# One store of attention's output and a copy by DMA, other queues for the last stores, and new plan numbers in an attention and mixture-of-experts kernel

## The chip, the cores and the metric

The kernel runs on one core of one Trainium2 chip. The metric is the device time of one execution in microseconds (us), the median of several runs. The kernel before takes 1061.25 us (three runs, 1060.74 to 1063.13).

## What is computed

Attention over 8 batches, 8 heads, 576 tokens and 64 columns a head, in which each query keeps its 32 largest scores, and behind it a mixture of 8 experts over all 4608 tokens. A token takes part only if its skip score is above zero, and goes to one expert.

```python
scores = scale * np.matmul(q, k.transpose(0, 1, 3, 2))
kth = np.partition(scores, -top_k, axis=-1)[..., -top_k:-top_k + 1]     # top_k = 32
scores = np.where(scores >= kth, scores, -1e9)
attn = np.exp(scores - max); attn /= sum + 1e-9
x = np.matmul(attn, v) -> rows of 512 columns, one row a token

do_compute = x @ w_skip > 0
e_idx = argmax(xc @ w_gate)                       # xc: the rows with do_compute
y[e_idx == e] = gate_w * (relu(xc @ w1[e]) @ w2[e])
out = x, and xc + y in the rows with do_compute
```

## The kernel before

Attention works on 32 pairs of heads (p), 4 pairs to a batch. For each pair, `load` and `load_v` bring q, k and v in (L85, L86, L505 to L510), `prep` turns q and k (L561) and swaps halves by DMA (tile TS, L584, L586), `rows` makes the scores of 9 row blocks (L619), finds each row's 32nd value with VectorE (L690 to L698), and marks the rest through ScalarE (L703, L716), GpSimd (L706, L710, L714) and VectorE (L719). `units` makes the scores again, turned and masked (L758 to L809), and `heads` multiplies by v (L850, L857), divides (L860, L888, L863, into the tile xb) and adds up the router's logits (L867 to L873).

The output of a pair goes from xb twice to DRAM: to XD, the table from which the experts gather their tokens, and to out. Each is one task `put` of four DMAs on SP's queue (L913, L914). For the last pair `put_last` (L906, L908) puts XD's four on ScalarE's queue and out's four on SP's.

When the four batches 0 to 3, the three batches 4 to 6, or batch 7 are complete, `route` ranks their tokens among the experts (L400 to L442), stores the gate weights into XD (`store`, L353 and L354; on ScalarE's queue for batch 7, else on SP's), and `lists`, once a batch, builds one-hots (rrh L461 and L466, lo1 in five parts L470) which TensorE multiplies into lists of tokens (L476, added up by VectorE at L479). For batches 0 to 6 the one-hots of L466 and L470 are GpSimd's; for batch 7 three of five parts and L466 are VectorE's (the function `on`).

The first two blocks of expert 0 need only batches 0 to 6: they are gathered on GpSimd (`gather`, L1026), turned (L1045, L1049 on ScalarE, L1053 on VectorE) and multiplied (`up` L1110 to L1112, `down` L1133 to L1135). Its third block and the other experts wait for batch 7's lists. The weights are split into two parts for the products by `part_hi` (L963, ScalarE) and `part_lo` (L966, VectorE), and fetched by L960 on SP. Expert outputs go to out by an indirect scatter (L1039).

The order on every engine is fixed when the kernel is built. A planner (`Plan`, `pick`, `run`) plays the work through with a duration and a due time for each task; each engine takes, of the tasks ready first, the one due first, and issues its instructions in that order. Due times are 9 a pair, plus a number for the kind of task (K, FINE); LOOK and GAIN say when an engine may wait for a more urgent task, TURN what a change of TensorE's kind of product costs. There are two runs of the plan: one ends with attention and the turning of expert 0's first blocks, the second holds batch 7's route, expert 0 and the turning for expert 1. Engines execute in order, and SP, which issues nearly all DMAs, waits in order too.

Of the kernel before, what the change touches and what calls it, by code (L numbers as in the profile page):

```python
# [32 lines left out]
LOOK, GAIN, KEEP = 0.027, 36.005, 0.000  # L33
DRAIN, TURN = 0.11, 28700.19
K = dict(ld=-546.563, turn=-120.465, put=-237.977, swap=-421.948, rr=33.73, rc=-49.731, qk=42.376, copy=-177.435, chunk=76.184, step=11.097, cand=-62.556, cstep=-187.113, sign=-8.081, fill=-185.335, push=-553.097, window=-5.964, pen=333.292, top=-210.867, flag=-156.199, unit=143.314, exp=-190.441, f1=70.038, f5=-98.317, lg=-208.068, co=298.059, ce=-33.501, rt=406.078, rd=63.598, rs=-191.199, moe=493.198, vt=-35.892, vp=-215.869, vg=-230.983, lv=-174.638, lr=-8.41)

FINE = dict(turn=(-249.498, -433.994, -337.654), put=(351.929, -329.073, -660.94), swap=(-41.128, -119.866, -577.692, -199.011), qk=(187.823, -221.268, 505.088, 511.446, 108.203), copy=(-246.306, -73.921, 287.494, -108.704, -278.328), chunk=(-24.303, -6.103, -7.999, 33.525, -39.857, -37.824, 1.877, 20.048, -67.673), cand=(5.33, -41.889, -480.491, -501.067, -1.709, -9.738, -282.518, -57.751, 36.539), sign=(481.767, 179.764, 7.521, 236.037, 144.293, 55.588, 387.412, 201.445, 493.783), fill=(4.812, -185.534, 211.624, 6.001, 13.752, 10.699, -0.796, 170.396, -154.693), push=(89.009, -290.332, 343.332, -115.781, 149.083, -72.663, -444.053, 220.923, -636.945), window=(-214.222, -578.183, 110.655, -507.736, -338.509, 68.646, 54.63, -121.054, -200.803), pen=(197.017, 233.591, -609.792, 155.04, 161.382, -368.212, 123.195, -300.258, 86.571), top=(132.194, 180.552, 274.851), unit=(-176.43, -402.794, 3.19, 161.712, 223.085, 129.562), exp=(-215.454, 342.652, -375.644, -329.678, 283.567, -477.568), f1=(102.089, -312.556, -403.168, -107.097, 72.352, -290.717, -487.223, 19.781, -483.104, 57.113, -224.605), f5=(-518.292, -303.227, -99.179, -77.179, -205.205, -250.298), lg=(372.735, -10.653), vt=(63.521, 158.904), vp=(-309.717, 192.783), vg=(-158.098, 364.353))
RS = 1.0
FILLS = True
# [4 lines left out]
def tile_kernel(ctx, tc, q, k, v, w_skip, w_gate, w1, w2, out):  # L44
# [303 lines left out]
    def store(b, xb, whats, due, after, end=False):  # L348

        q = nc.scalar if end else nc.sync  # L350

        def f(dst, u, w):
            q.dma_start(dst[b * S:b * S + MAIN, u:w].rearrange("(p t) c -> p t c", p=P), xb()[:, 0:NM])  # L353
            q.dma_start(dst[b * S + MAIN:(b + 1) * S, u:w], xb()[0:REM, NM])  # L354
        return [pl.add("ACT" if end else "SP", 0.15 if end else 1.35, due, lambda x=x: f(*x), after, lag=2.5) for x in whats]

    def route(bs, wk, due, bank=BT):
# [88 lines left out]
        on = lambda late: ("DVE", 0.2, V_) if late and end else ("POOL", 0.61, nc.gpsimd)  # L446
        listed = [None, None, bx]

        def lists(j):
# [14 lines left out]
            for k, a in enumerate((ta, tb)):  # L464
                e, dur, eng = on(True)
                u.append(pl.add(e, min(dur, 0.39), due, lambda k=k, a=a, eng=eng: eng.tensor_tensor(  # L466
                    L["rh"][:, :, k], L["rh"][:, :, 2], bl(a), op=OP.mult), x))
# [214 lines left out]
    def row(p, t):  # L682
# [52 lines left out]
        fx = A("POOL" if FILLS else "DVE", 0.25 if FILLS else 0.129, W_("fill"), fill, rr, old)  # L735
# [91 lines left out]
    def heads(p):  # L827
# [10 lines left out]
        def values(a):  # L838
# [53 lines left out]
            for j in range(4 if a else 1):  # L892
                x = A(on, 0.1 if end else 0.25, when(p, "lg", a), lambda j=j: logit(j), x, LGFREE[-1:])
                LGFREE.append(x)
                logits.append(x)
# [8 lines left out]
        def put_last(dst, a, q):  # L904
            c0 = hp * P + a * D
            q.dma_start(dst[b * S:b * S + MAIN, c0:c0 + D].rearrange("(p t) d -> p t d", p=P), xb[:, a, 0:NM, 0:D])  # L906
            for h in range(2) if a else ():
                q.dma_start(dst[b * S + MAIN:(b + 1) * S, hp * P + h * D:hp * P + (h + 1) * D], xb[hs_(h), 1, NM, 0:D])  # L908

        def put(dst):  # L910
            q, c0 = nc.sync, hp * P
            for h in range(2):
                q.dma_start(dst[b * S:b * S + MAIN, c0 + h * D:c0 + (h + 1) * D].rearrange("(p t) d -> p t d", p=P), xb[:, h, 0:NM, 0:D])  # L913
                q.dma_start(dst[b * S + MAIN:(b + 1) * S, c0 + h * D:c0 + (h + 1) * D], xb[hs_(h), 1, NM, 0:D])  # L914
        if end:
            STORES[p] = [A("ACT", 0.6 + 1.2 * a, due, lambda a=a: put_last(XD, a, nc.scalar), done[a], lag=2.5) for a in range(2)]
            for a in range(2):
                A("SP", 0.6 + 1.2 * a, due, lambda a=a: put_last(out, a, nc.sync), STORES[p][a], lag=2.5)
        else:
            STORES[p] = [A("SP", 1.35, due, lambda dst=dst: put(dst), done, lag=2.5) for dst in (XD, out)]  # L920
# [583 lines left out]
```

## Time and profile before

| | us |
|---|---|
| median of three runs | 1061.25 |
| the profiled execution, its own time | 1061.84 |
| its span, from the first to the last instruction | 1059.9 |
| TensorE busy | 1004.0 |
| VectorE busy | 898.6 |
| ScalarE busy | 862.2 |
| GpSimd busy | 706.7 |

Attention takes the span up to about 804 us, the experts the rest. A busy share over the whole span mixes the two: in attention TensorE, VectorE and ScalarE are all nearly full, behind it TensorE alone is. In the rows below, times are microseconds from the start of the span; in a row of the timeline the first number is the start, the second the duration, x how many instructions are merged, and the bracket at the end how long the engine stood idle before it and what released it. PE is TensorE, DVE VectorE, ACT ScalarE, POOL GpSimd, SPq and ACTq the DMA issues of SyncE and ScalarE.

### The profile page before, as it was taken

How to read it: one execution, taken by the hardware profiler on the slowest of the kernel's cores; microseconds unless marked ns; L12 is line 12 of the kernel's file. 1: busy time of each engine (PE TensorE's matmuls, PEld its weight loads, DVE VectorE, ACT ScalarE, POOL GpSimd, SP SyncE). 2: the span in 40 equal slices, each digit the busy share in tenths (PEclk: the TensorE clock that was granted, in tenths of full speed). 3: DMA queues.
4: the chain of work that ended last, by engine and by line, in shares of the span. 5: the costliest groups of instructions: out<-in, count | busy, mean ns of one | idle time of the engine just before them, and what ended most of it. 6: DMA issues, size and time to landing. Idle time of an engine off the chain costs nothing.

```text
span 1059.9 us, 40100 instructions
## 1 busy us (share of the span) xinstructions
PE 1004.0 (95%) x14932; PEld 714.4 (67%) x14932; DVE 898.6 (85%) x4914; ACT 862.2 (81%) x1548; POOL 706.7 (67%) x1074
## 2 busy tenths in 40 slices
PE   6889999999999999998999899999997999999996
PEld 3456666666666657665666566666676999888995
DVE  5999999999999999997999899999875666674661
ACT  5999999999999999997999899999993354434540
POOL 3878878888777888886779898888993222210210
PEclk9899999999999999998999899999998999999998
DMA  4433444444444434434354444554226275554720
GB/s 111 98 85 80 92 95 96 91 105 97 97 94 94 92 90 100 104 86 87 88 120 113 114 105 98 118 131 90 60 49 198 74 249 168 169 161 165 210 80 29
DMA packets 290092, 116.16 MB, mean 110 GB/s; under 512 B 258920, under 2 KB 275304, under 8 KB 289888
## 3 DMA queue, kind: packets, MB, share of 16 engines
q1 hardware_dynamic: 283504, 103.42, 39.9%
q0 software_dynamic: 3360, 9.47, 2.7%
q8 instruction: 120, 1.97, 0.8%
q10 hardware_dynamic: 3024, 0.61, 0.3%
q14 instruction: 84, 0.69, 0.2%
HBM read 76.91 MB, written 24.53 MB: 96 GB/s over the span
## 4 chain that ended last, share of the span: by engine, by line
PE 54%; DVE 14%; POOL 13%; ACT 11%; issue 4%; DMA 2%; SPq 1%; ACTq 0%; POOLq 0%; DVEq 0%
PE r L619 7%; POOL xw L706 7%; PE r L767 6%; DVE cand L690 6%; PE pa L850 5%; PE pt L850 4%; PE ph L1110 4%; PE ph L1111 4%; PE ph L1112 4%; DVE wn L719 3%; PE py L1133 3%; PE py L1135 3%; ACT r L703 3%; PE py L1134 3%; POOL xw L710 2%
## 5 line engine op out<-in xcount | busy, mean ns | idle before, releaser
L706 POOL TENSOR_TENSOR xw<-XC,r 128x576 f32<-128x576 f32 x288 | 364.8, 1281 | 84.1 <-ACT r L703 53.6
L690 DVE MAX8 cand<-XC 128x8 f32<-128x82 f32 (+1 forms) x2016 | 359.1, 229 | 15.1 <-ACT XC L647 14.4
L703 ACT ACTIVATE r<-XC,cl 128x576 bf16<-128x576 f32 x288 | 226.4, 793 | 7.0 <-DVE cl L696 3.4
L719 DVE MAX8 wn<-xw 128x8 f32<-128x585 f32 x288 | 215.0, 760 | 16.6 <-POOL xw L710 13.4
L619 PE MATMUL r<-TT 64*64 64x64 f32 (+1 forms) x1280 | 198.8, 426 | 1.6 <-ACT PTM L800 0.8
L716 ACT ACTIVATE PEN<-XC,wn 128x576 bf16<-128x576 f32 x225 | 171.5, 791 | 3.0 <-DVE wn L719 2.5
L619 PE MATMUL r<-TS 64*64 64x512 f32 (+1 forms) x1024 | 158.8, 422 | 3.1 <-DMA TS<-TT 3.1
L696 DVE MAX8 cl<-cand 128x8 f32<-128x42 f32 (+2 forms) x864 | 158.1, 191 | 0.9
L767 PE MATMUL r<-TT 64*128 64x512 f32 (+1 forms) x528 | 147.8, 638 | 9.2 <-ACT XC L649 7.4
L800 ACT ACTIVATE PTM<-r,top 128x1024 f32<-128x1024 f32 x124 | 137.3, 1123 | 4.0 <-PE r L758 3.9
L647 ACT ACTIVATE XC<-r 128x1024 f32<-128x1024 f32 x128 | 132.0, 1037 | 7.0 <-PE r L619 6.8
L758 PEld LDWEIGHTS <-PEN 64*128 64x128 bf16 (+1 forms) x2880 | 70.9, 99 | 72.9 <-issue 68.3
L714 POOL TENSOR_SCALAR PEN<-XC,wn 128x576 bf16<-128x576 f32 x63 | 108.8, 1729 | 12.9 <-DVE wn L719 2.7
L710 POOL TENSOR_SCALAR xw<-wo,CN 128x9 f32<-128x9 f32 x288 | 98.6, 343 | 26.0
L698 DVE MATCH_REPLACE8 cand<-cl,cand 128x28 f32<-128x28 f32 (+1 forms) x576 | 102.0, 180 | 0.0
L850 PEld LDWEIGHTS pa<-VG,PTM 128*64 128x64 f32 x2048 | 72.6, 138 | 28.1 <-ACT PTM L800 5.7
L850 PEld LDWEIGHTS pt<-VG,PTM 128*64 128x64 f32 x2048 | 72.7, 138 | 27.5 <-ACT PTM L800 8.0
L619 PEld LDWEIGHTS r<-TT 64*64 64x64 f32 x1280 | 59.5, 134 | 45.2 <-issue 29.0
L1110 PE MATMUL ph<-xh,hi 128*128 128x224 f32 (+4 forms) x288 | 85.9, 298 | 3.6 <-DVE xl L1053 3.6
L850 PE MATMUL pt<-VG,PTM 128*64 128x74 f32 x2048 | 83.3, 232 | 3.5 <-DVE xb L863 1.7
L850 PE MATMUL pa<-VG,PTM 128*64 128x74 f32 x2048 | 83.8, 232 | 2.8 <-DVE xb L863 1.7
L1026 POOL DMA_INDIRECT xg<-xd,idx x21 | 23.3, 1112 | 93.9 <-DVE ot L1032 85.3
(257 smaller groups left out, 2058.8 us busy)
## 6 DMA issues: line engine op xcount, KB each, us to landing
wb<-in_moe_w_dram SPq DMA_DIRECT2D x32, 512.0 KB, 7.3
raw<-in_moe_w_dram SPq DMA_DIRECT2D x28, 512.0 KB, 3.4
TS<-TT SPq DMA_DIRECT2D x64, 144.0 KB, 2.5
raw<-in_k_dram SPq DMA_DIRECT2D x64, 128.0 KB, 3.2
VG<-in_v_dram SPq DMA_DIRECT2D x64, 128.0 KB, 2.6
vraw<-in_v_dram SPq DMA_DIRECT2D x64, 128.0 KB, 2.7
out_dram<-xb SPq DMA_DIRECT2D x64, 128.0 KB, 2.3
raw<-in_q_dram SPq DMA_DIRECT2D x62, 128.0 KB, 2.7
```

The costliest lines, as they stand in the source:

```text
L619: nc.tensor.matmul(o[hs_(h)], q_, (ts[src, u:w] if y else tt[src, 0, u:w]), start=True, stop=True)
L647: nc.scalar.activation(xc[:, t:u + 1:u - t, 0:MAIN], h2.t.rearrange("p (y c) -> p y c", y=2), AF.Copy)
L690: nc.vector.max(C_[:, c], xc[:, CH[c]:CH[c + 1]])
L696: nc.vector.max(L[:, 4 * r:4 * r + 8], c)
L703: nc.scalar.activation(rr_, xc, AF.Sign, bias=CL[p % 2][:, t, 23:24], scale=-ODD, accum_out=CN[:, s:s + 1])
L706: nc.gpsimd.tensor_tensor(xw[:, 0:S], xc, rr_, op=OP.mult)
L716: nc.scalar.activation(pen, xc, AF.Relu, bias=WN[p % 2][:, t, 7:8], scale=-1.0)
L719: nc.vector.max(WN[p % 2][:, t], xw)
L767: nc.tensor.matmul(rb[:, 512 * h + u:512 * h + w], tt[hs_(h), 0, REM + P * kc:REM + P * (kc + 1)], tt[hs_(h), 1, REM + u:REM + w], start=T ...
L800: nc.scalar.activation(o_.rearrange("p h c -> p (h c)"), i_, AF.Exp, bias=nb, scale=scale)
L850: nc.tensor.matmul(h.t[hs_(t % 2), VW * (t // 2):VW * (t // 2 + 1)], w, vg[:, a, kc], start=(kc == 0 and t < 2), stop=(kc == NM), skip_gro ...
L1110: nc.tensor.matmul(ph[:, u:w], h1[:, c], xh[:, c, u:w], start=(c == 0), stop=False)
```

## The change

A pair's output is stored once, to XD: one DMA as soon as the first half of xb is done, three DMAs for the second half. A further task on SP copies the pair's 576 rows of 128 columns from XD to out with one DMA from DRAM to DRAM, which waits for those stores and is due 12 behind them. The last pair has no stores of its own kind any more; they and batch 7's gate stores are on SP. The one-hots of L466 and of three of the five parts of L470 are VectorE's for batches 4 to 6 too. The plan's durations for several tasks are set to other values (fill, logits, one-hots, stores), and all its due numbers and LOOK, GAIN and TURN are new.

```diff
-LOOK, GAIN, KEEP = 0.027, 36.005, 0.000
-DRAIN, TURN = 0.11, 28700.19
+LOOK, GAIN, KEEP = 0.026, 6.352, 0.000
+DRAIN, TURN = 0.11, 86667984302.89
...
-        q = nc.scalar if end else nc.sync
+        q = nc.sync
...
-        return [pl.add("ACT" if end else "SP", 0.15 if end else 1.35, due, lambda x=x: f(*x), after, lag=2.5) for x in whats]
+        return [pl.add("SP", 0.15 if end else 1.35, due, lambda x=x: f(*x), after, lag=2.5) for x in whats]
...
-        on = lambda late: ("DVE", 0.2, V_) if late and end else ("POOL", 0.61, nc.gpsimd)
+        on = lambda late: ("DVE", 0.2, V_) if late and b0 + nb >= B - 1 else ("POOL", 0.61, nc.gpsimd)
...
-                u.append(pl.add(e, min(dur, 0.39), due, lambda k=k, a=a, eng=eng: eng.tensor_tensor(
+                u.append(pl.add(e, dur if end else 0.36 if e == "POOL" else 0.25, due, lambda k=k, a=a, eng=eng: eng.tensor_tensor(
...
-        fx = A("POOL" if FILLS else "DVE", 0.25 if FILLS else 0.129, W_("fill"), fill, rr, old)
+        fx = A("POOL" if FILLS else "DVE", 0.40 if FILLS else 0.129, W_("fill"), fill, rr, old)
...
-                x = A(on, 0.1 if end else 0.25, when(p, "lg", a), lambda j=j: logit(j), x, LGFREE[-1:])
+                x = A(on, 0.1 if end else 0.28, when(p, "lg", a), lambda j=j: logit(j), x, LGFREE[-1:])
...
-        def put_last(dst, a, q):
+        def put(a):
             c0 = hp * P + a * D
-            q.dma_start(dst[b * S:b * S + MAIN, c0:c0 + D].rearrange("(p t) d -> p t d", p=P), xb[:, a, 0:NM, 0:D])
+            nc.sync.dma_start(XD[b * S:b * S + MAIN, c0:c0 + D].rearrange("(p t) d -> p t d", p=P), xb[:, a, 0:NM, 0:D])
             for h in range(2) if a else ():
-                q.dma_start(dst[b * S + MAIN:(b + 1) * S, hp * P + h * D:hp * P + (h + 1) * D], xb[hs_(h), 1, NM, 0:D])
-
-        def put(dst):
-            q, c0 = nc.sync, hp * P
-            for h in range(2):
-                q.dma_start(dst[b * S:b * S + MAIN, c0 + h * D:c0 + (h + 1) * D].rearrange("(p t) d -> p t d", p=P), xb[:, h, 0:NM, 0:D])
-                q.dma_start(dst[b * S + MAIN:(b + 1) * S, c0 + h * D:c0 + (h + 1) * D], xb[hs_(h), 1, NM, 0:D])
-        if end:
-            STORES[p] = [A("ACT", 0.6 + 1.2 * a, due, lambda a=a: put_last(XD, a, nc.scalar), done[a], lag=2.5) for a in range(2)]
-            for a in range(2):
-                A("SP", 0.6 + 1.2 * a, due, lambda a=a: put_last(out, a, nc.sync), STORES[p][a], lag=2.5)
-        else:
-            STORES[p] = [A("SP", 1.35, due, lambda dst=dst: put(dst), done, lag=2.5) for dst in (XD, out)]
+                nc.sync.dma_start(XD[b * S + MAIN:(b + 1) * S, hp * P + h * D:hp * P + (h + 1) * D], xb[hs_(h), 1, NM, 0:D])
+
+        def copy_out():
+            bs, cs = slice(b * S, (b + 1) * S), slice(hp * P, (hp + 1) * P)
+            nc.sync.dma_start(out[bs, cs], XD[bs, cs])
+        STORES[p] = [A("SP", 0.62 + 1.24 * a, due, lambda a=a: put(a), done[a], lag=2.5) for a in range(2)]
+        A("SP", 0.64, due + 12.0, copy_out, STORES[p], lag=2.5)
```

## Rows read from the trace of the kernel before

**Rows 1.** The page's busy times: time, share of the span, instructions of each engine.

```profile
PE 1004.0 (95%) x14932; PEld 714.4 (67%) x14932; DVE 898.6 (85%) x4914; ACT 862.2 (81%) x1548; POOL 706.7 (67%) x1074
```

**Rows 2.** Busy time of engines by stretch, with length, granted clock, DMA share, GB/s.

```profile
100.00:400.00 300.00, 292.88 (x5281) 190.46 (x5279) 291.72 (x1815) 297.82 (x546) 247.41 (x355) 1.00 0.43 95
400.00:760.00 360.00, 346.49 (x6196) 225.10 (x6192) 340.24 (x2105) 345.75 (x634) 303.92 (x461) 0.98 0.45 103
490.00:510.00 20.00, 15.58 (x252) 10.20 (x248) 12.92 (x86) 13.04 (x26) 11.93 (x19) 0.83 0.49 105
590.00:610.00 20.00, 16.96 (x278) 11.40 (x271) 17.89 (x111) 17.37 (x34) 17.36 (x27) 0.83 0.41 102
...
810.00:815.00 5.00, 5.00 (x27) 5.00 (x27) 4.21 (x9) 3.15 (x6) 0.00 (x0) 0.55 1.08 354
```

**Rows 3.** Timeline of SP's DMA issues before 492 us.

```profile
474.92 0.62 SPq L913 DMA_DIRECT2D xd<-xb  x1
...
489.77 0.64 SPq L354 DMA_DIRECT2D xd<-gt  x1
490.45 1.29 SPq L85 DMA_DIRECT2D raw<-in_k_dram  x2
491.79 0.63 SPq L86 DMA_DIRECT2D rawr<-in_k_dram  x1
```

**Rows 4.** Timelines of PE, ACT and DVE in the same place.

```profile
494.63 0.45 PE L561 MATMUL pt<-identF,rawr 128*128 128x128 f32 x1 [4.42 <-issue]
...
495.11 0.28 ACT L568 ACTIVATE TT<-pt 128x128 f32<-128x128 f32 x1 [4.19 <-PE pt L561]
...
498.11 0.25 DVE L690 MAX8 cand<-XC 128x8 f32<-128x83 f32 x1 [4.23 <-ACT XC L647]
```

**Rows 5.** DMA issues by line: count, size, median us from issue to landing.

```profile
out_dram<-xb SPq DMA_DIRECT2D x64, 128.0 KB, 2.3
...
xd<-xb SPq DMA_DIRECT2D x62, 128.0 KB, 3.0
```

**Rows 6.** Timelines of POOL and PE at attention's end.

```profile
797.11 0.21 PE L476 MATMUL r<-rrh,rlo 128*128 128x72 bf16 x1 [0.37 <-POOL rlo L470]
...
788.41 2.92 POOL L470 TENSOR_SCALAR rlo<-i,rank 128x128 bf16<-128x128 f32 x5
...
793.38 3.67 POOL L470 TENSOR_SCALAR rlo<-i,rank 128x128 bf16<-128x128 f32 x5
...
800.27 1.34 POOL L1026 DMA_INDIRECT xg<-xd,idx  x1 [1.04 <-DVE idx L1015]
```

**Rows 7.** Timeline of DVE: batch 7's one-hots.

```profile
825.90 0.48 DVE L466 TENSOR_TENSOR rrh<-rrh,tabs 128x120 bf16<-128x120 bf16 x2
826.29 0.67 DVE L470 TENSOR_SCALAR rlo<-i,rank 128x128 bf16<-128x128 f32 x3
```

**Rows 8.** Timelines of PE, ACT and DVE between attention and expert 0.

```profile
803.54 0.33 PE L857 MATMUL pt<-VG,PR 128*64 128x74 f32 x4
...
809.75 0.56 PE L1110 MATMUL ph<-xh,hi 128*128 128x224 f32 x1 [3.61 <-DVE xl L1053]
...
806.12 1.55 ACTq L908 DMA_DIRECT2D xd<-xb  x2
807.77 1.08 ACT L1049 ACTIVATE xh<-r 128x512 fp32r<-128x512 f32 x2 [5.14 <-DMA xd<-xb]
...
805.98 0.16 DVE L873 TENSOR_TENSOR lg<-lg,lgr 64x9 f32<-64x9 f32 x1
808.40 1.29 DVE L1053 TENSOR_TENSOR xl<-r,xh 128x512 fp32r<-128x512 f32 x2 [2.27 <-ACT xh L1049]
809.61 0.18 DVE L400 TENSOR_REDUCE rmx<-lg 128x5 f32<-128x40 f32 x1
```

**Rows 9.** Timelines of POOL and PE where expert 0's third block comes in.

```profile
829.59 1.10 POOL L1026 DMA_INDIRECT xg<-xd,idx  x1 [4.68 <-DVE ranked L993]
...
835.61 0.33 PE L1111 MATMUL ph<-xl,hi 128*128 128x128 f32 x1 [0.23 <-DVE xl L1053]
```

More of the change, by code (lines that the diff above doesn't have):

```diff
@@ L32 @@
         ("PE", "PE"): 0.0}
-LOOK, GAIN, KEEP = 0.027, 36.005, 0.000
-DRAIN, TURN = 0.11, 28700.19
-K = dict(ld=-546.563, turn=-120.465, put=-237.977, swap=-421.948, rr=33.73, rc=-49.731, qk=42.376, copy=-177.435, chunk=76.184, step=11.097, cand=-62.556, cstep=-187.113, sign=-8.081, fill=-185.335, push=-553.097, window=-5.964, pen=333.292, top=-210.867, flag=-156.199, unit=143.314, exp=-190.441, f1=70.038, f5=-98.317, lg=-208.068, co=298.059, ce=-33.501, rt=406.078, rd=63.598, rs=-191.199, moe=493.198, vt=-35.892, vp=-215.869, vg=-230.983, lv=-174.638, lr=-8.41)
@@ L37 @@
-FINE = dict(turn=(-249.498, -433.994, -337.654), put=(351.929, -329.073, -660.94), swap=(-41.128, -119.866, -577.692, -199.011), qk=(187.823, -221.268, 505.088, 511.446, 108.203), copy=(-246.306, -73.921, 287.494, -108.704, -278.328), chunk=(-24.303, -6.103, -7.999, 33.525, -39.857, -37.824, 1.877, 20.048, -67.673), cand=(5.33, -41.889, -480.491, -501.067, -1.709, -9.738, -282.518, -57.751, 36.539), sign=(481.767, 179.764, 7.521, 236.037, 144.293, 55.588, 387.412, 201.445, 493.783), fill=(4.812, -185.534, 211.624, 6.001, 13.752, 10.699, -0.796, 170.396, -154.693), push=(89.009, -290.332, 343.332, -115.781, 149.083, -72.663, -444.053, 220.923, -636.945), window=(-214.222, -578.183, 110.655, -507.736, -338.509, 68.646, 54.63, -121.054, -200.803), pen=(197.017, 233.591, -609.792, 155.04, 161.382, -368.212, 123.195, -300.258, 86.571), top=(132.194, 180.552, 274.851), unit=(-176.43, -402.794, 3.19, 161.712, 223.085, 129.562), exp=(-215.454, 342.652, -375.644, -329.678, 283.567, -477.568), f1=(102.089, -312.556, -403.168, -107.097, 72.352, -290.717, -487.223, 19.781, -483.104, 57.113, -224.605), f5=(-518.292, -303.227, -99.179, -77.179, -205.205, -250.298), lg=(372.735, -10.653), vt=(63.521, 158.904), vp=(-309.717, 192.783), vg=(-158.098, 364.353))
@@ new lines @@
+LOOK, GAIN, KEEP = 0.026, 6.352, 0.000
+DRAIN, TURN = 0.11, 86667984302.89
+K = dict(ld=-665.624, turn=-294.211, put=-160.163, swap=-358.812, rr=15.77, rc=-46.279, qk=159.612, copy=-5.616, chunk=65.783, step=7.819, cand=-158.488, cstep=-187.63, sign=11.403, fill=-141.096, push=-499.803, window=-3.908, pen=369.361, top=-210.962, flag=33.507, unit=192.182, exp=-160.426, f1=171.73, f5=-379.762, lg=-231.384, co=282.166, ce=19.07, rt=345.117, rd=148.173, rs=-447.813, moe=626.704, vt=155.686, vp=-186.981, vg=-320.687, lv=-220.575, lr=-19.092)
@@ new lines @@
+FINE = dict(turn=(-366.736, -634.098, -404.912), put=(216.077, -300.742, -867.113), swap=(-218.257, -250.229, -562.08, -210.477), qk=(292.243, -262.088, 352.101, 484.898, 27.898), copy=(-323.805, -220.221, 159.421, -177.437, -301.124), chunk=(-30.041, -33.338, 26.764, 61.63, -61.379, -58.647, -5.036, 17.049, -87.646), cand=(27.661, 17.891, -527.6, -542.288, -122.83, 111.441, -189.969, 13.881, 34.608), sign=(445.812, 187.864, 32.606, 218.714, 128.713, 121.369, 264.558, 221.619, 499.752), fill=(-41.807, -230.109, 225.875, 28.27, 57.436, 44.538, -24.072, 114.702, -175.062), push=(45.98, -387.537, 352.018, -87.688, 209.337, -109.418, -466.447, 193.169, -712.073), window=(-222.595, -593.193, 115.041, -457.851, -347.732, 74.368, 53.86, -22.538, -307.082), pen=(246.824, 432.902, -620.663, 287.683, 318.64, -529.283, 90.984, -471.764, 60.217), top=(139.995, 30.715, 317.049), unit=(-166.709, -371.885, -25.199, 329.457, 339.255, 305.622), exp=(-289.038, 344.611, -495.138, -433.771, 254.325, -446.067), f1=(58.774, -375.738, -668.119, -137.23, 71.463, -396.315, -493.07, -91.968, -571.16, 40.73, -249.58), f5=(-438.051, -218.375, -131.461, 263.169, -283.144, -338.662), lg=(416.756, 50.643), vt=(-96.056, -31.256), vp=(-489.313, 162.425), vg=(-180.822, 259.859))
```

## The prediction

> **What bounds the kernel now.** I read the page's busy times first, then busy time by stretch, then the timelines of the places where a stretch falls off. The page has TensorE busy for 95% of the span [rows 1], but that mean hides two stages. In attention three engines are full together: between 100 and 400 us ScalarE is busy 297.82 of 300, TensorE 292.88, VectorE 291.72 [rows 2]. So the steady state has only 2.2 us of ScalarE to give back, and none of the edits takes work from these three engines there. What can move is the places where all three stop at once. From 400 to 760 us ScalarE is idle 360 - 345.75 = 14.2 us, where the pace of 100 to 400 would leave 2.6; so 11.6 us are lost. Two places hold most of it: 490 to 510 (7.0 us idle on ScalarE, 4.4 on TensorE, granted clock 0.83) and 590 to 610 (2.6 us, again 0.83) [rows 2].
>
> The first place is SP's. TensorE waits 4.42 us for a turn of `rawr`, and ScalarE (4.19) and VectorE (4.23) stop behind it [rows 4]. The profile names only "issue", but SP's timeline shows it: the load of that tile was issued at 491.79 and TensorE went on 2.2 us after that issue was through; the loads had stood behind 20 issues that began at 474.92, 8 of them stores of one pair's output, 8 gate stores, 4 loads of v [rows 3]. SP had no gap there. Eight issues of some 0.63 us are 5.0 us, where the plan booked 2 x 1.35 = 2.7: the plan believed the loads to be over 2 us earlier than they were.
>
> The third place is between attention and expert 0. Attention's last product ends at 803.54 + 0.33 = 803.87, the first `up` starts at 809.75 [rows 8]. From there TensorE has no gap until the third block comes at 835.61, where it waits 0.23 us [rows 9]: expert 0's first two blocks just cover batch 7's route. From then on TensorE is the only bound, and nothing in the change touches its work.
>
> **The change part by part.** *Stores and plan times.* A pair has 5 DMA issues instead of 8; at 0.62 to 0.64 [rows 3] SP gains 3 x 0.63 = 1.9 us a pair. Beside other work that is worth nothing: loads land early in most pairs. On the path it counts where SP has no gap, at 490. There the load moves 1.9 us up by itself, and with bookings of 0.62 + 1.86 + 0.64 = 3.1 us for five issues, which is what they take, the plan can place the loads ahead of gate stores, which nobody awaits for long. Bounds: nothing, if the new order again piles up gate stores and loads; the 7.0 us of ScalarE at most. I take 5.0, as 4.4 us of TensorE's wait and the lower clock behind it hang on that one load. The second place has another cause (banks and turns in sequence), so a new order removes it or makes one like it: 2.6 us either way; I take 0.5 for it and all the rest. Fill, logit and one-hot durations only change the order. Attention's term is -5.5; its bounds are -11.6 (everything runs as between 100 and 400) and +4.5 (the first place stays, a second one like 590 and some more come up).
>
> The copy's bytes are an extra read of 4608 x 512 x 4 = 9.4 MB, at a DMA share of 0.43 to 0.45 [rows 2], and the rows it writes are 512 bytes where xb's were 256; hidden. What covers this is that nobody reads `out` before the scatters, behind the third block. The wait it adds stands on SP: the copy may go only when the stores have landed, 3.0 us after issue [rows 5], and behind it in SP's queue stand the loads and swaps of the next pairs, for which TensorE waits. The due time is 12 later than the stores', and the plan books a lag of 2.5; so I cost it at nothing, with 0 to 3 us in a pair where SP reaches it early. That is a rival below.
>
> *One-hots.* For batches 4 to 6 GpSimd gives up 9 of 15 parts of L470 (3.67 / 5 = 0.73 and 2.92 / 5 = 0.58 each [rows 6]) and 6 of L466; VectorE takes them at 0.22 and 0.24 [rows 7]: 9 x 0.22 + 6 x 0.24 = 3.4 us. Part of that falls where VectorE is full, up to 1.6 us for the first two lists; GpSimd gets about twice that back in the same place, and it feeds the last rows. The last list is on the path now: its parts end at 797.05, TensorE waits four times 0.37 us for them, and the gathers start only at 800.27 [rows 6]. With three of five parts elsewhere it ends some 3 x 0.73 + 2 x 0.35 = 2.9 us earlier, and the gathers, turns, xh and xl of expert 0's first blocks can come before attention's last products. Gain at attention's end: 1.5 us for the four waits, up to 1.5 more from GpSimd's relief, against up to 1.3 for turns that now stand ahead; I take 1.5 (0 to 3).
>
> *Last stores off ScalarE.* Its four issues run until 806.12 + 1.55 = 807.67, and xh stands behind them (5.14 us, put down to `xd<-xb`), xl behind xh, and in VectorE's order the first step of batch 7's route (L400, 809.61) behind xl, though its logits were done at 805.98 + 0.16 = 806.14 [rows 8]. That is 3.47 us of the route, which sets the third block; all of it goes. The four issues on SP now stand ahead of the fetch of expert 1's weights, with the copy and its wait of 3.0 us; those weights are used behind the third block, so this is hidden. Batch 7's gate stores on SP delay fetches of the same kind.
>
> The trace shows four issues holding ScalarE for 3.2 us at the worst place. The Trainium skill, "DMA: Bandwidth & Descriptors", section "Issuing engines are not separate DMA queues", says that starting DMAs on several engines saves only the sequencer's time to start them, usually small. By that rule this move gains next to nothing and could cost; the sum would be -5.0 us. The row disagrees here: the sequencer's time is what xh waits for.
>
> *What is late next.* The third block then comes at 835.61 - 3.47 - 1.5 = 830.6. TensorE's covering work was 809.75 to 835.4 = 25.7 us, of which the 5 us at granted clock 0.55 [rows 2] held about 2.1 us of slowness; so 23.6 us. Started at 803.87 - 1.5 = 802.4 it ends at 826.0, and TensorE stands idle for 4.6 us. After the gaps of 4.42 and 3.61 us the clock was at the lower level [rows 2, 4, 8], so the third block pays about 2 us back (0 to 2.1). The transition's term: -3.47 - 1.5 + 2 = -3.0, bounds -7 and 0.
>
> **Sum.** 1061.84 (the profiled execution: span 1059.9 and 1.9 around it) - 5.5 - 3.0 = 1053.3. That execution lies 0.6 above the median of the runs; so 1052.7.
>
> **Rivals.**
> *1. The loop becomes even.* All 11.6 us come back, and the transition gives 5: 1061.25 - 16.6 = 1044.7. For it: 300 us of the same work do run at that pace. Against it: a new order over 32 pairs rarely has no bad place.
> *2. The gain moves.* The place at 490 goes, others like it come, and only the transition stays: 1058.2; with a transition of 0, 1061. For it: every due number changed, and 590 shows that stops arise without SP.
> *3. Slower: the copy stops SP.* If SP comes to a copy right behind its stores, it stands up to 3.0 us with the next pair's loads behind it. SP has room for that in an ordinary pair (23 issues x 0.63 = 14.5 us, plus 3.0, of 803.87 / 32 = 25 us a pair), so it decides only where SP has no gap, as around 490 where gate stores pile up. One such stop costs what 490 to 510 shows, 7.0 us; if the old one stays as well, and the transition brings 3: 1061.25 + 7 - 3 = 1065. The Trainium skill, same page, "Two DMAs through the same engine are not ordered", says that one queue gives no order and that the issuing engine must wait for the first DMA's semaphore; no run here shows what happens without.
> *4. It does not do what it says:* the copy is not hidden, and scatters wait for it. The last copy would be issued at about 811, 20 us before the third block; this costs nothing and gets no chance.
>
> **How the numbers follow.** A change under 0.2% (2.1 us) cannot be told from none. Forecast (1048 to 1058) 0.52; rival 1 0.14; rival 2 0.18, half of it still faster by more than 2.1 us; rival 3 0.16. Faster: 0.52 + 0.14 + 0.09 = 0.75. Same: 0.09. Slower: 0.16. The range runs from 1043 to 1063: it takes in rival 1 but its lowest part, rival 2, and the mild end of rival 3.
>
> **What would show it.** SP's timeline with no row of 20 issues ahead of a load for which TensorE waits; no stretch of 20 us in attention with ScalarE under 18; xh and xl before attention's last product, and the first `up` within 1 us of it; L400 right behind the last L873; a gap of TensorE before the third block, near 5 us. Wrong would be: the same or a new stop of all engines in the loop, SP waiting at the copy's line, or a third block that is no earlier relative to attention's end than 835.61 - 803.87 = 31.7 us.

## The result and the profile after

The changed kernel takes 1051.93 us, the median of four runs (1050.56 to 1053.55), beside 1061.37 for the kernel before on the same chip: a ratio of 0.9909 (95% interval 0.989 to 0.9928). The prediction was 1052.7, within 1043 to 1063. The profiled execution took 1051.28, its span 1049.4 (before: 1061.84 and 1059.9).

First the page of the changed kernel: busy time, share, instructions; what HBM moved; the new copy's issues, their size and time to landing. The engines are as busy in us as before [rows 1]. HBM reads 86.35 MB where it read 76.91: the 9.44 MB of the copy.

```profile
PE 1001.8 (95%) x14932; PEld 713.5 (68%) x14932; DVE 898.4 (86%) x4929; ACT 861.9 (82%) x1548; POOL 700.7 (67%) x1059
...
HBM read 86.35 MB, written 24.53 MB: 106 GB/s over the span
...
out_dram<-xd SPq DMA_DIRECT2D x32, 288.0 KB, 3.3
```

Next busy time by stretch of the changed kernel, columns as in [rows 2].

```profile
100.00:400.00 300.00, 296.04 (x5315) 192.58 (x5309) 289.05 (x1807) 297.99 (x545) 245.12 (x355) 1.00 0.43 96
400.00:760.00 360.00, 350.49 (x6346) 229.01 (x6342) 344.92 (x2160) 353.29 (x650) 312.74 (x469) 1.00 0.45 102
490.00:510.00 20.00, 20.00 (x377) 13.21 (x369) 19.50 (x123) 19.99 (x37) 18.49 (x29) 1.00 0.44 87
590.00:610.00 20.00, 18.61 (x296) 11.29 (x296) 18.99 (x105) 19.91 (x37) 18.17 (x28) 1.00 0.43 108
680.00:700.00 20.00, 16.35 (x266) 10.31 (x264) 18.81 (x136) 15.94 (x31) 17.95 (x30) 0.91 0.56 126
```

The steady stretch is as full as it was. Both bad places of [rows 2] are even now. From 400 to 760 ScalarE is idle 6.7 us instead of 14.2, so 7.5 came back. But a place of the same kind stands at 680 to 700 (4.06 us idle on ScalarE), and there TensorE waits for GpSimd's one-hots of batches 0 to 3 and then for ScalarE:

```profile
692.02 0.21 PE L476 MATMUL pt<-rrh,rlo 128*128 128x72 bf16 x1 [0.69 <-POOL rlo L470]
692.59 0.21 PE L476 MATMUL pt<-rrh,rlo 128*128 128x72 bf16 x1 [0.37 <-POOL rlo L470]
694.56 1.73 PE L767 MATMUL r<-TT 64*128 64x512 f32 x4 [1.76 <-ACT XC L649]
```

SP's timeline of the changed kernel before 490 answers [rows 3]. Ahead of the load at 487.23 stand 12 issues (the eight loads of v from 471.70, three stores, one copy), and SP then stands still for 5.3 us until that load's buffer is free. The queue is no longer what the load waits for.

```profile
471.70 0.59 SPq L505 DMA_DIRECT2D VG<-in_v_dram  x1
...
478.68 1.27 SPq L908 DMA_DIRECT2D xd<-xb  x2
481.34 0.56 SPq L912 DMA_DIRECT2D out_dram<-xd  x1
487.23 1.28 SPq L85 DMA_DIRECT2D raw<-in_q_dram  x2
```

Last the way from attention to expert 0 in the changed kernel, timelines of PE, ACT, DVE and POOL. Of [rows 6, 8, 9], L1039 answers L1045 (turn), L1043 L1049 (xh), L1047 L1053 (xl), L1104 L1110 (`up`), L1020 L1026 (gather).

```profile
793.22 0.30 PE L857 MATMUL pt<-VG,PR 128*64 128x74 f32 x4
794.81 0.63 PE L1039 MATMUL r<-identF,xg 128*128 128x128 f32 x4 [1.29 <-POOL hl L1116]
796.34 0.66 PE L1039 MATMUL r<-identF,xg 128*128 128x128 f32 x4 [0.90 <-DMA xg<-xd,idx]
798.40 0.55 PE L1104 MATMUL ph<-xh,hi 128*128 128x224 f32 x1 [1.41 <-DVE xl L1047]
...
824.79 0.33 PE L1105 MATMUL ph<-xl,hi 128*128 128x128 f32 x1 [0.22 <-DVE xl L1047]
...
797.03 0.60 ACT L1043 ACTIVATE xh<-r 128x512 fp32r<-128x512 f32 x1 [0.90 <-PE r L1039]
...
796.77 0.15 DVE L873 TENSOR_TENSOR lg<-lg,lgr 64x9 f32<-64x9 f32 x1
797.66 0.69 DVE L1047 TENSOR_TENSOR xl<-r,xh 128x512 fp32r<-128x512 f32 x1 [0.74 <-ACT xh L1043]
798.27 0.18 DVE L400 TENSOR_REDUCE rmx<-lg 128x5 f32<-128x40 f32 x1
...
791.00 1.34 POOL L1020 DMA_INDIRECT xg<-xd,idx  x1 [4.05 <-issue]
```

The first `up` still waits for a chain from the gather to xl, and comes 798.40 - 793.52 = 4.88 us behind attention's end (before 5.88). The third block follows the work ahead of it with 0.22 us of a gap.

The same points in all kernels that follow, in us from the span's start, read from the timelines. The last product of L676 closes the loop's regular part; attention's end is the end of its last product with v (L850 or L857); "third block" is its first `up`.

| | last L676 | attention's end | first gather | logits done | first `up` | third block |
|---|---|---|---|---|---|---|
| before | 781.81 | 803.87 | 800.27 | 806.13 | 809.75 | 835.07 |
| after | 774.21 | 793.52 | 791.00 | 796.92 | 798.40 | 824.26 |
| before, no stores to out | 775.91 | 796.29 | 794.37 | 799.75 | 802.32 | 827.65 |
| before, last stores on SP | 782.83 | 804.76 | 801.30 | 806.71 | 808.58 | 833.32 |
| before, one-hots on VectorE | 793.04 | 811.12 | 799.14 | 813.96 | 812.39 | 837.29 |
| after, last stores on ScalarE | 775.87 | 795.20 | 792.68 | 798.62 | 800.65 | 826.01 |
| after, one-hots on GpSimd | 775.04 | 794.10 | 798.63 | 798.21 | 809.51 | 835.42 |
| after, zeroing on ScalarE | 774.55 | 792.22 | 789.30 | 794.59 | 797.44 | 823.61 |
| after, zeroing on ScalarE, index first | 776.34 | 794.03 | 789.60 | 798.39 | 798.05 | 825.15 |

So of the 10.8 us, 7.6 come before the last L676, 2.8 between it and attention's end (22.06 to 19.31), and 0.5 between attention's end and the third block (31.20 to 30.74).

Each row is one execution. The five kernels "after" in this table give SP, ScalarE, VectorE and GpSimd the same order of work up to 768 us, and their last L676 still differ by 2.1 us. So a difference of 1 or 2 us between two rows is no effect by itself; distances within one row say more.

Most of the 2.8 is TensorE's clock. Busy times from the last L676 to attention's end, before and after, and in the kernel without stores to out:

```profile
781.81:803.87 22.06, 18.65 (x347) 14.87 (x346) 10.87 (x23) 15.21 (x24) 20.26 (x46) 0.92 0.14 35
774.21:793.52 19.31, 16.46 (x347) 13.53 (x346) 15.55 (x43) 13.71 (x21) 14.30 (x24) 1.00 0.15 35
775.91:796.29 20.38, 16.98 (x347) 13.79 (x346) 10.98 (x24) 15.21 (x24) 18.58 (x32) 1.00 0.05 12
```

The same 347 products keep TensorE busy 18.65 us before and 16.46 after, and its idle time falls from 3.41 to 2.85 us. Before, the granted clock was 0.50 (the lower level, 1.2 GHz) from 797.4 to 800.8, behind the four waits for the last list [rows 6], and 1.00 (2.4 GHz) in the rest. The waits alone do not decide it: the kernel without stores to out has the same four, and its clock stayed at 1.00.

### The profile page after: what moved, and what is told of

Its sections match the earlier page's. It is cut to its first block, busy times and chain, and to the rows that moved or that the text cites. A ratio compares the mean times of both kernels' runs of the same rounds, so it can differ in the third digit from the quotient of the medians.

```text
span 1049.4 us, 39975 instructions
## 1 busy us (share of the span) xinstructions
PE 1001.8 (95%) x14932; PEld 713.5 (68%) x14932; DVE 898.4 (86%) x4929; ACT 861.9 (82%) x1548; POOL 700.7 (67%) x1059
## 3 DMA queue, kind: packets, MB, share of 16 engines
HBM read 86.35 MB, written 24.53 MB: 106 GB/s over the span
## 5 line engine op out<-in xcount | busy, mean ns | idle before, releaser
L690 DVE MAX8 cand<-XC 128x8 f32<-128x82 f32 (+1 forms) x2016 | 364.5, 229 | 10.9 <-ACT XC L647 10.2
L703 ACT ACTIVATE r<-XC,cl 128x576 bf16<-128x576 f32 x288 | 227.8, 796 | 3.3 <-DVE cl L696 3.0
L619 PE MATMUL r<-TS 64*64 64x512 f32 (+1 forms) x1024 | 156.2, 418 | 5.1 <-DMA TS<-TT 4.4
L696 DVE MAX8 cl<-cand 128x8 f32<-128x56 f32 (+2 forms) x864 | 156.4, 190 | 0.5
L850 PEld LDWEIGHTS pt<-VG,PTM 128*64 128x64 f32 x2432 | 84.6, 137 | 29.7 <-ACT r L703 8.1
L850 PE MATMUL pt<-VG,PTM 128*64 128x74 f32 x2432 | 97.0, 231 | 2.8 <-DVE xb L863 0.9
L1020 POOL DMA_INDIRECT xg<-xd,idx x21 | 23.6, 1124 | 98.8 <-DVE ot L1026 86.9
L1104 PE MATMUL ph<-xh,hi 128*128 128x224 f32 (+4 forms) x288 | 86.2, 299 | 1.4 <-DVE xl L1047 1.4
L1105 PE MATMUL ph<-xl,hi 128*128 128x224 f32 (+4 forms) x288 | 85.8, 298 | 0.2 <-DVE xl L1047 0.2
L1106 PE MATMUL ph<-xh,lo 128*128 128x224 f32 (+4 forms) x288 | 85.6, 297 | 0.0
```

What stands on the lines that cost most here:

```text
L619: nc.tensor.matmul(o[hs_(h)], q_, (ts[src, u:w] if y else tt[src, 0, u:w]), start=True, stop=True)
L690: nc.vector.max(C_[:, c], xc[:, CH[c]:CH[c + 1]])
L696: nc.vector.max(L[:, 4 * r:4 * r + 8], c)
L703: nc.scalar.activation(rr_, xc, AF.Sign, bias=CL[p % 2][:, t, 23:24], scale=-ODD, accum_out=CN[:, s:s + 1])
L850: nc.tensor.matmul(h.t[hs_(t % 2), VW * (t // 2):VW * (t // 2 + 1)], w, vg[:, a, kc], start=(kc == 0 and t < 2), stop=(kc == NM), skip_gro ...
```

## The experiments

### The place at 490 and SP's queue

**The kernel before without the loop's stores to out.**

```diff
-            for h in range(2):
+            for h in range(2) if dst is XD else ():
```

> The kernel before, with the four stores of each pair to the output left out (all but the last pair's); the plan books them as before, so every engine keeps its order, and only SP has four issues less a pair, some 2.5 us. Its output lacks attention's rows. Theory A (SP's queue makes the stop near 490 us): the load for which TensorE waits is issued about 2.5 us earlier, the wait of 4.4 us shrinks to about 2, and the kernel is 3 to 6 us faster than before, so 1055 to 1058. Theory B (the stop comes from the order of work on the other engines): the stop stays and the time is within 1 us of before, 1060 to 1062.

Measured 1057.1, ratio 0.9949 (0.993 to 0.9968): 4.8 us less by the medians. The profiled execution is the fastest of five (1054.86; the slowest took 1059.65). In it the starts of the marks of the 288 row blocks (L703) stay within 0.25 us of the kernel before up to 283 us, slip 1.0 us near 291, and then gain 6.25 us in one step, between the marks at 490.0 and 505.7 of the kernel before. Later steps are small: 1.0 gained between 601 and 617, 0.55 lost at 661. The wait for the turn of `rawr` is 0.85 us instead of 4.42, with another releaser, and in the busy times by stretch the place is gone:

```profile
491.83 0.30 PE L561 MATMUL pt<-identF,rawr 128*128 128x128 f32 x1 [0.85 <-ACT r L703]
```

```profile
490.00:510.00 20.00, 19.15 (x364) 12.50 (x360) 18.29 (x107) 19.18 (x36) 16.86 (x29) 1.00 0.47 106
```

The queue was the cause of this stop, and its price is 6.25 us in this execution. Elsewhere in the loop four issues fewer a pair do little.

**The changed kernel with four stores from xb in place of the copy.**

```diff
-            nc.sync.dma_start(out[bs, cs], XD[bs, cs])
+            for h in range(2):
+                c0 = hp * P + h * D
+                nc.sync.dma_start(out[... MAIN rows ..., c0:c0 + D], xb[:, h, 0:NM, 0:D])
+                nc.sync.dma_start(out[... last rows ..., c0:c0 + D], xb[hs_(h), 1, NM, 0:D])
```

> The changed kernel, but in place of the one copy from the table to the output SP issues four stores from xb, booked in the plan at the same 0.64 us; the order on the other engines is the changed kernel's. Theory A (fewer issues on SP are part of the gain): 1.9 us more of SP a pair, unknown to the plan, bring back waits of TensorE for loads; 4 to 9 us slower than the changed kernel, 1056 to 1061. Theory B (the gain is the new order alone): within 2 us of the changed kernel, 1050 to 1054.

Measured 1059.04, ratio 0.9959 (0.9936 to 0.9982): 7.1 us of the 9.4 are lost by the medians, some 5.3 by the ratios. The profiled execution is the slowest of nine (1061.42; the fastest took 1053.83). In it the marks fall behind the changed kernel's by 4.2 to 6.3 us between 273 and 497, by 11.9 from 522 on, and by 10.4 at the end. The order is the same, only each pair has three issues more than SP's plan books. The largest step is a stop like that at 490, now at 521: four stores to out stand right ahead of the load, from 513.87.

```profile
518.90 0.63 SPq L86 DMA_DIRECT2D rawr<-in_k_dram  x1
...
521.58 0.45 PE L561 MATMUL pa<-identF,rawr 128*128 128x128 f32 x1 [2.87 <-issue]
```

No engine waits for a store to out there, so it is not xb being held longer. So the small number of issues matters, in more than one place of the loop.

**The kernel before with the copy, in its old place in the order.**

```diff
+            if dst is out:
+                q.dma_start(out[b * S:(b + 1) * S, c0:c0 + P], XD[b * S:(b + 1) * S, c0:c0 + P])
-            for h in range(2):
+            for h in range(2) if dst is XD else ():
```

> The kernel before, in which the second store of a pair (four DMAs to the output) is the copy from the table instead, in the same place and booked alike, so right behind the stores it waits for; the other engines keep their order. SP has three issues less a pair (1.9 us) and a wait for the landing. Theory C (the copy's wait stops SP where it has no gap, the slower rival): 2 to 3 us of wait a pair undo the 1.9, the load near 490 us is not earlier, and the time is 1061 to 1066. Theory D (the wait is shorter than the three issues, as the first of the four stores have landed by then): 2 to 4 us faster than before.

Measured 1061.26, ratio 1.0002 (0.9984 to 1.002). The timelines of SP and TensorE, and then SP's waits (us in total, times, longest), show where the three issues saved went:

```profile
478.49 0.62 SPq L916 DMA_DIRECT2D xd<-xb  x1
480.64 0.56 SPq L913 DMA_DIRECT2D out_dram<-xd  x1
...
490.12 1.29 SPq L85 DMA_DIRECT2D raw<-in_k_dram  x2
...
494.81 0.45 PE L561 MATMUL pt<-identF,rawr 128*128 128x128 f32 x1 [4.43 <-DMA rawr<-in_k_dram]
```

```profile
SPq L913 <- DMA xd<-xb: 54.3, 31, 3.4
```

SP stands 480.64 - 479.11 = 1.53 us for the stores to land, nearly the 1.9 us that three issues take, and TensorE's wait is 4.43 us as before. Over the loop it waits 31 times, 54.3 us in all. With the copy due 12 later, as in the changed kernel, it is 22 times and 25.7 us, with 2.5 the longest, at no place that TensorE waits for; SP's waits of the changed kernel have it as

```profile
SPq L912 <- DMA xd<-xb: 25.7, 22, 2.5
```

In its old place the copy pays nothing.

**The kernel before with batches 0 to 3's gate stores due 100 us later.**

```diff
-... [(XD, DM, DM + 8)], due + 0.9 + 0.2 * j, gx, end)
+... [(XD, DM, DM + 8)], due + (100.0 if nb == B // 2 else 0.9) + 0.2 * j, gx, end)
```

> The kernel before with the gate stores of batches 0 to 3 due 100 us later, nothing left out. Theory A (the stop at 490 is the sum of what stands on SP's queue there, so any eight issues fewer remove it, as leaving the output's stores out did): one step of 4 to 7 us at 490 and no other change, 1055 to 1057.5. Theory B (gate stores are put in by the plan where SP is free, the output's stores alone make the stop): no step at 490, 1061 to 1062. Theory C (the stores pile up 100 us later and make the same stop there): the step at 490 and a new stop near 590, 1059 to 1062.

Measured 1061.91, ratio 1.0002 (0.9988 to 1.0016), and the step is still there. But this says nothing against the queue, for the gate stores did not leave it. SP's order up to 768 us is that of the kernel before:

```profile
483.32 0.56 SPq L353 DMA_DIRECT2D xd<-gt  x1
...
492.10 1.29 SPq L85 DMA_DIRECT2D raw<-in_k_dram  x2
...
496.98 0.45 PE L561 MATMUL pt<-identF,rawr 128*128 128x128 f32 x1 [4.48 <-issue]
```

A due time ranks, in this planner, only those tasks that are ready together; where SP is free in the plan, a store goes at once however late it is due. Whether the gate stores alone would make the stop stays open.

### Due numbers and tasks

**The changed kernel with the due numbers of before, and the kernel before with the new ones.**

```diff
-LOOK, GAIN, KEEP = 0.026, 6.352, 0.000
+LOOK, GAIN, KEEP = 0.027, 36.005, 0.000
```

(with TURN, K and FINE; the other kernel has the reverse)

> The changed kernel with the due numbers, LOOK, GAIN and TURN of the kernel before. Theory A (stores, booked times, queue and one-hots make the gain, due numbers only shuffle): at least 6 of the 9.4 us stay, 1052 to 1056. Theory B (the new due numbers make it): the gain of attention goes and only its end's 2.7 us stays, 1058 to 1061.

> The kernel before with the due numbers, LOOK, GAIN and TURN of the changed kernel, and nothing else. Theory A: SP is still booked at half its time, stops like that at 490 us remain somewhere in attention, 1058 to 1066. Theory B: attention's gain of about 7 us comes with the due numbers, 1053 to 1056.

Measured 1385.54 (ratio 1.3033, 1.301 to 1.3056) and 1111.23 (1.0458, 1.0433 to 1.0484). In the first the engines wait for each other everywhere; from its waits:

```profile
POOL xw L706 <- ACT r L703: 248.7, 80, 12.7
...
PE pa L676 <- DVE cl L696: 146.5, 13, 12.5
```

The second stays within 7 us of the kernel before for 180 of 288 marks, and is 35 to 43 us behind it from 577 on. No theory had these numbers. The due numbers of either kernel do not fit the other's tasks and durations, so the gain cannot be divided between them by exchanging them.

### Last stores

**The kernel before with the last stores on SP; the changed kernel with them on ScalarE.**

```diff
-        q = nc.scalar if end else nc.sync
+        q = nc.sync
...
-        return [pl.add("ACT" if end else "SP", 0.15 if end else 1.35, due, ...
+        return [pl.add("SP", 0.15 if end else 1.35, due, ...
...
-            STORES[p] = [A("ACT", 0.6 + 1.2 * a, due, lambda a=a: put_last(XD, a, nc.scalar), ...
+            STORES[p] = [A("SP", 0.6 + 1.2 * a, due, lambda a=a: put_last(XD, a, nc.sync), ...
```

> The kernel before, with the last pair's stores to the table and the last gate stores on SP instead of ScalarE, nothing else. Prediction's step (the four issues on ScalarE cost the route 3.47 us): about 3.5 us faster, 1057.5 to 1059. Rival (the second gather lands only just before, so xh can start 1.6 us earlier and no more): 1 to 2 us faster. A third (starting DMAs elsewhere saves nothing): no change or slower.

> The changed kernel with the last pair's stores and the last gate stores on ScalarE, as they were before. Prediction's step: about 3.5 us slower, 1055. Rival (in the changed kernel xh waits for the gathers until 795.5 and 797.0, and the issues on ScalarE would end at about 797.0): 0 to 1 us slower, 1052 to 1053.

The first: 1059.23, ratio 0.998 (0.9965 to 0.9995). From attention's end to the third block it takes 28.56 us instead of 31.20, so 2.64 are gained, 2.06 of them ahead of the first `up`; attention itself ends 0.9 later. The second: 1053.82, ratio 0.9944 (0.9925 to 0.9962), 1.9 slower than the changed kernel by the medians; the two intervals touch. In the trace only 0.1 lies behind attention's end (30.81 beside 30.74). The other 1.7 are there at the last L676 already, most of it by 230 us, far from the edit and with the same order on SP, ScalarE, VectorE and GpSimd: they are no more than two executions of one order differ. ScalarE's timeline tells why the stores cost nothing there:

```profile
797.93 1.30 ACTq L908 DMA_DIRECT2D xd<-xb  x2
799.27 0.60 ACT L1043 ACTIVATE xh<-r 128x512 fp32r<-128x512 f32 x1 [1.45 <-PE r L1039]
```

Here xh waits for the turn, which waits for the gather; the four issues fit into that wait. In the kernel before the gathers were early and xh waited for the issues [rows 8].

### One-hots

**The changed kernel with the one-hots of batches 4 to 6 on GpSimd.**

```diff
-        on = lambda late: ("DVE", 0.2, V_) if late and b0 + nb >= B - 1 else ("POOL", 0.61, nc.gpsimd)
+        on = lambda late: ("DVE", 0.2, V_) if late and end else ("POOL", 0.61, nc.gpsimd)
```

> The changed kernel with all one-hots of L466 and L470 of batches 4 to 6 on GpSimd again. Theory (one-hots on VectorE bring attention's end 2.7 us forward and the gathers with it): 2 to 4 us slower, 1054 to 1056, attention's last product some 3 us later behind the last top. Rival (VectorE's gain is eaten by its own weight halves, the gathers wait for idx all the same): within 1 us.

Measured 1062.65, ratio 1.0026 (1.0003 to 1.0048): 10.7 us slower than the changed kernel, more than the whole gain. Attention's end hardly moves (794.10 beside 793.52). GpSimd's and TensorE's timelines, and busy time in one stretch:

```profile
782.30 4.57 POOL L470 TENSOR_SCALAR rlo<-i,rank 128x128 bf16<-128x128 f32 x5
...
787.55 4.72 POOL L470 TENSOR_SCALAR rlo<-i,rank 128x128 bf16<-128x128 f32 x5
...
800.24 1.00 POOL L1020 DMA_INDIRECT xg<-xd,idx  x1 [0.31 <-issue]
...
807.73 1.09 PE L1039 MATMUL r<-identF,xg 128*128 128x128 f32 x4 [3.08 <-DMA xg<-xd,idx]
```

```profile
804.00:808.00 4.00, 0.93 (x6) 0.55 (x5) 0.69 (x1) 0.60 (x1) 0.00 (x0) 0.50 1.08 372
```

GpSimd builds the three lists one behind the other from 781.09 to 795.86, and the first gather is 7.6 us later. The second is issued at 800.24, beside the 2 MB fetch of expert 1's weights (SP issues it from 799.85), and its tile is there at 807.73, 7.5 us later; in the changed kernel 792.64 to 796.34 are 3.7. The granted clock is 0.50 meanwhile, the lower level, and the turn takes 1.09 instead of 0.66. So the first `up` comes 11.1 us later.

**The kernel before with those one-hots on VectorE.**

```diff
-        on = lambda late: ("DVE", 0.2, V_) if late and end else ("POOL", 0.61, nc.gpsimd)
+        on = lambda late: ("DVE", 0.2, V_) if late and b0 + nb >= B - 1 else ("POOL", 0.61, nc.gpsimd)
```

(with the bookings of L466 of the changed kernel)

> The kernel before with one part of the change alone: the late one-hots of batches 4 to 6 on VectorE, with their bookings. Theory A (their worth is that the gathers come before attention's end; in the kernel before they already stand at 800.27, 3.6 us ahead of attention's end at 803.88, and the first product waits for ScalarE's stores): the gathers come some 5 us or more earlier, the first product not, and the time gains at most the 1.5 us of TensorE's four waits: 1060 to 1061.5. Theory B (the one-hots are worth some 11 us wherever they stand, as taking them back from the changed kernel cost): 1050 to 1053. Theory C (VectorE is full, so 3.4 us of work more on it costs that much): 1063 to 1065.

Measured 1062.39, ratio 1.001 (0.9994 to 1.0027): the 11 us are not there. The gathers do come early, at 799.14, 12.0 us ahead of attention's end, and a turn stands ahead of attention's last products, as the prediction had it for the changed kernel. But attention ends 7.25 us later (1.6 of it is there at 761 already). The other 5.6 are as much as these one-hots take on VectorE (5.65); they stand ahead of the last pair's search, and TensorE waits for it.

```profile
783.75 0.74 PE L857 MATMUL pt<-VG,PTR 128*64 128x74 f32 x16 [2.29 <-ACT PTR L805]
...
792.70 0.77 PE L676 MATMUL pa<-shift,top 128*128 128x128 f32 x2 [4.63 <-DVE top L677]
```

The same edit is worth nothing in the old order and 10.7 us in the new one. By these two it pays where the lists are the last thing that expert 0 waits for and VectorE has room.

### Zeroing on ScalarE

**The changed kernel with the gather buffers zeroed by ScalarE instead of GpSimd.**

```diff
-    y = pl.add("POOL", 1.6, D0, lambda: nc.gpsimd.memset(XG[0], 0.0), room)
+    y = pl.add("ACT", 1.5, D0, lambda: nc.scalar.activation(XG[0]..., identF[:, 0:1].to_broadcast(...), AF.Copy, scale=0.0), room)
```

(and XG[1] in the same way, further back in the order)

> The changed kernel with the two zeroings of the gathered tiles (1560 columns, 1.4 us each) on ScalarE instead of GpSimd. In the changed kernel three parts of the one-hots take VectorE 2.05 us instead of 0.67 while GpSimd zeroes, and a copy of 9 columns 1.04 us instead of 0.17. Theory (VectorE is held by GpSimd's zeroing): both shrink to 0.7 and 0.2, TensorE's wait of 1.09 us for the last list goes, the gathers start 1 to 2 us earlier, and the kernel is 1 to 3 us faster. Rival (VectorE was slow for another reason): the times stay.

Measured 1049.77, ratio 0.9886 (0.9865 to 0.9907). The first gather is 1.7 us earlier, the third block 0.65. TensorE's wait of 1.09 us for the last list is gone. It is the shortest of all kernels here, but its interval overlaps that of the changed kernel, so that it is faster than that one is not shown. VectorE's rows of the changed kernel beside GpSimd's, and below "..." VectorE's with the zeroing gone:

```profile
785.05 2.05 DVE L470 TENSOR_SCALAR rlo<-i,rank 128x128 bf16<-128x128 f32 x3
795.01 1.04 DVE L871 COPY lgr<-xb 64x9 f32<-64x9 f32 x1
785.56 1.39 POOL L1081 MEMSET xg<- 128x1560 f32 x1
794.59 1.42 POOL L1117 MEMSET xg<- 128x1560 f32 x1
```

```profile
785.36 0.70 DVE L470 TENSOR_SCALAR rlo<-i,rank 128x128 bf16<-128x128 f32 x3
...
794.22 0.17 DVE L871 COPY lgr<-xb 64x9 f32<-64x9 f32 x1
```

**The same, with three of the four L960 of expert 0's first weights put behind the index of the gathers.**

```diff
-        PARTED.append(pl.add("DVE", 1.22, D0 + 1 + i, lambda i=i: part_lo(0, i), x))
+        PARTED.append(pl.add("DVE", 1.22, D0 + 1 + i, lambda i=i: part_lo(0, i), x, idxx if i else None))
```

> The same, and three of the four weight halves of L960 on VectorE wait for the list's index (L1007 to L1009), so that the gathers go first. Theory (after the one-hots the index stands behind 1.21 us weight halves, and the gathers set the first product): the gathers start 2 to 3 us earlier against attention's end than in the changed kernel, first product within 3 us of attention's last; another 1 to 2 us faster. Rival (the third block is set by batch 7's route, which starts at the last logits): at most 1 us faster than the version with the zeroings alone.

Measured 1051.26, ratio 0.9899 (0.9871 to 0.9927). Against attention's end the first gather is 1.5 us earlier than without this edit (4.43 ahead instead of 2.92) and the first `up` 1.2 (4.02 behind instead of 5.22), but the third block only 0.3 (31.12 instead of 31.39). In this execution the last L676 is at 776.34, 1.8 later than without the edit; the order up to 768 us is the same, so this is a difference between executions (the runs go from 1046.31 to 1054.89). A gain is not shown.

## Why the prediction was right, and where it was not

**The time and the first cause were right.** The stop at 490 was SP's queue, and its price was between what I took (5.0) and the 7.0 that I gave as its most: 6.25 as a step in one execution of the kernel without the stores, while its medians, with everything else in them, give 4.8. That the short booking let the queue pile up was argued and not tried: no run has the kernel before with true bookings alone. The loop's term was -7.6 instead of -5.5, within its bounds. The 7.5 us of ScalarE's idle time that came back between 400 and 760 are the same number from the other side.

**The rest of the loop** went as the step said, "removes it or makes one like it": 590 went and 680 to 700 came. So the sign that no stretch of 20 us has ScalarE under 18 was wrong (15.94). How the new due numbers and durations do this is not taken apart; they work with these tasks only.

**The copy** was hidden, as costed. Rival 3 had its mechanism right and its place wrong: in the old order the landing wait does eat what the issues save (1.0002), and in the new order, with the copy due 12 us behind its stores, the waits fall where SP has room. That the due time alone does this was not tried.

**The one-hots are a step that failed.** I sized them at 1.5 us and put the gain at attention's end. Taking them back moves that end by 0.6 us, no more than two executions of one order differ, and the first `up` by 11.1, through the gathers. The gathers were ready 3.6 us ahead of attention's end in the kernel before, and so I did not ask what they cost once attention ends 10 us sooner. The price on VectorE was mis-sized too: the nine L470 of batches 4 to 6 take 3.85 us and the six L466 1.63, together 5.5, not 3.4, since I priced them by batch 7's rows [rows 7], where GpSimd does nothing beside them.

**The last stores** were priced at 3.47, as time of a route "which sets the third block". That step failed too: the route does not set it. From the first `up` to the third block TensorE has no gap in either kernel, 25.32 us before and 25.86 after, and the route's products stand in its order and are not waited for. In the kernel before, the first of them comes 2.3 us behind its input (VectorE's row, then TensorE's); in the changed kernel it is 2.3 again.

```profile
817.01 0.19 DVE L408 TENSOR_TENSOR roh<-wts,m 128x40 bf16<-128x40 f32 x1
...
819.50 0.19 PE L416 MATMUL px<-roh,tri 128*128 128x40 bf16 x1
```

So these stores are worth what they bring the first `up` forward: xh did wait for them in the kernel before, and there, with them on SP, the first `up` comes 2.06 us nearer to attention's end and the third block 2.64; the other 0.58 is TensorE's clock behind the first `up`, 0.93 instead of 0.91. In the changed kernel the third block gains 0.1. I had weighed the Trainium skill's rule ("DMA: Bandwidth & Descriptors", section "Issuing engines are not separate DMA queues") that starting DMAs on several engines saves only the sequencer's time, usually small. It fits the changed kernel; in the kernel before that time was on the path and not small. The row decides only as long as its engine's next instruction waits for nothing else.

**What is late next** I had wrong. The gathers did not come ahead of attention's last products: they are issued 2.5 us before its end (3.6 before), the first `up` stands 4.9 behind it and not within 1, and the gap before the third block is 0.22 us, not near 5, since TensorE's own work sets that block. L400 is not right behind the last L873, either: it waits 798.27 - 796.92 = 1.35 for xl, and the logits themselves are done 3.40 us behind attention's end instead of 2.26, of which 0.87 is the copy L871 that GpSimd's zeroing holds. The first `up` came 1.0 us nearer to attention's end, and 0.5 of it went again: TensorE spent 5.77 us at a granted clock of 0.50 behind it, where it had been 4.74. Hence 0.5 where the sum had 3.47 less 2.

**The errors cancel.** That the transition's sum came out is luck: it was to bring 3.0 and brought 3.2, but 2.8 of them ahead of attention's end (predicted 1.5). 2.2 of the 2.8 are TensorE's busy time, with the clock at 1.00 where it had been 0.92, which the sum did not have; 0.6 is idle time. The one-hots are not the cause: with them on GpSimd again the clock there is 1.00 too, and that stretch takes 19.06 us. What in the new order keeps the clock up is open. With the loop's 2.1 more, that is the whole difference between the predicted 8.5 and the 10.8 in the trace. The medians differ by only 9.4, since the profiled execution of the kernel before lay 0.5 above its median of 1061.37 and that of the changed kernel 0.65 below its own.

## What to carry to other kernels

Where a fixed order books a queue's issues too short, look for the place where that queue has no gap: the price is there, in one step, and the count of issues times their duration tells how much has to go. A copy that waits for its own stores must stand well behind them in the queue, or its wait takes back what it saves. What an engine's work near a transition is worth has to be asked again with the transition where the rest of the change puts it: the same one-hots were worth nothing in one order and 11 us in the other. And where an engine runs without a gap up to a point, that engine sets the point: a chain that feeds it, like the route here, is worth nothing until the engine waits for it.

## What the runs showed of the hardware

Some of VectorE's instructions are held while GpSimd zeroes a tile. The copy L871 takes 0.17 us alone and 1.04 beside a zeroing of GpSimd's, ending at 796.05 as the zeroing ends at 796.01; three L470 take 0.70 and 2.05. It goes both ways: in the kernel with the one-hots on GpSimd five L470 take 4.57 and 4.72 us while VectorE splits weights (L960) in part of that time, and 2.91 behind it. Not everything is held: in the kernel with the zeroing on ScalarE three L470 of VectorE's take 0.70 us beside GpSimd's L470, four of which take 3.70 there, and VectorE's L966 takes 1.22 us beside a zeroing in the kernel before (797.50 beside 797.21), as it does alone. The Trainium skill, "SBUF — State Buffer", section "Who interferes with whom", has this as an exclusive lock on a pair of ports that VectorE's copies and tensor_scalar operations share with GpSimd, while an operation with two inputs collides only with a GpSimd instruction that reads. These rows agree with it.

In one execution, the tile of a gather issued beside a fetch of 2 MB was there 7.5 us after its issue instead of 3.7, while the DMA engines were full (372 GB/s).
